# Moving stores of activated tiles and of prepared weight factors to GpSimd's queue, with two forms given later

## The chip, the cores and the metric

The kernel runs on one core of a Trainium2 chip. The core's engines are named as the profile names them: PE (TensorE matmul), PEld (its weight load), DVE (VectorE), ACT (ScalarE), POOL (GpSimd), SP (SyncE). "ACTq", "SPq" stand for what those engines' instruction queues do besides arithmetic, issuing DMAs above all. The metric is the device time of one execution in microseconds; the kernel before took 1059.97 us, the median of three runs (1058.99 to 1065.47).

## The reference

Three layers follow one another, in float32. First a retention over 4 batches, 8 heads, 768 positions and 64 features per head: a state per head is decayed and updated, and read with the query. The result, reshaped to 3072 tokens by 512 features, goes through two feed-forward layers of inner width 2048, the weights of which are given as 64-bit floats.

```python
state = gamma * state + k_t outer v_t          # y_t = scale * q_t @ state
x = y.transpose(0, 2, 1, 3).reshape(3072, 512)
h = x @ w_in;  x = np.maximum(0.01 * h, h) @ w_out        # first layer
h = x @ w_in2; y = (h * sigmoid(1.702 * h)) @ w_out2      # second layer
```

## The kernel before

A float32 product is made as three matmuls of values that are split into a rounded high part and the rest: ACT makes the high part (`nc.scalar.copy`), DVE subtracts it from the source. Layer products after the first columns are made by a seven-product scheme on half blocks (Strassen's manner): the products take sums of blocks, and those of the input are called forms 1 to 7.

The stages in order of time: the retention (`retention`, to about 134 us) with the first 512 columns of the first layer's inner products put between its steps (`ffn_in`, L244); a plain phase of 16 tiles (L948) for columns 512 to 767 by the same `ffn_in`; the first layer's input products by seven products (`first1`, class `First`, L533, to about 355 us); its output products (`second1`, class `Second`); and the same two for the second layer (`first2`, about 590 to 825 us, and `second2`).

In `First.run` the work goes over pairs (block of 768 columns, q of 8). A pair has seven groups of six matmuls of 384 columns each, and after each group comes a tick of a clock (`Later`), which calls steps that were put down for that tick; `beside` then calls at most one piece of the preparation of later weights (class `Prep`: a load, integer and float steps on ACT and DVE that turn 64-bit floats to float32, sums on DVE, a store). The first1 stage starts a `Prep` every 5 ticks, first2 every 7. Each engine runs its instructions in the order in which the program gives them. In a pair, `L672` is the ACT copy of the first product's PSUM bank to a second bank, and the later products into either bank come behind it. `inner` (L600) activates each of a pair's four results (`gate`, ACT, L618 for the gated layer and L620 for the other) into a tile of a ring of eight and stores it to DRAM (`store`, L608) on ACT's queue.

The DMA issues that the change touches: `factors_out` (L215, ACT; 8 times in the retention, the 512 KB tile `made` that POOL's subtractions of L157 write), `ffn_in`'s store (L257, ACT; in the retention and in the plain phase), `inner`'s store (L609, ACT) and `Prep.store` (L455, SP; 448 KB of prepared factors). SP's queue also issues the loads: L558 (a block of the layer's input, in four parts at the first block), L439 and L436 (raw weights), L898 (factors back from DRAM), L733 (activated tiles back for `Second`).

The forms of first1's first block are put down in the plain phase (`early_steps`, L941): form 7 at its last tile (L945), and form 3 in `step1` at the first pair (L958). `First.form` (L567) takes the ticks at which its subtraction of blocks, the ACT copy (L577) and the DVE subtraction come. The block sums that forms 5 and 6 start from are made by DVE at L563 and L565.

Of the kernel before, what the change touches and what calls it, by code (L numbers as in the profile page):

```python
# [22 lines left out]
B, H, S, D = 4, 8, 768, 64  # L23
# [4 lines left out]
TB = 512  # L28
# [3 lines left out]
NQ = KF // 2  # L32
# [58 lines left out]
def retention_two_ffn(ctx: ExitStack, tc: tile.TileContext, qkv, consts, small, w1i, w1o, w2i, w2o, scratch, out):  # L91
    nc = tc.nc
# [37 lines left out]
    wd = {kind: dram.tile([P, NQ, 2, 7, P], F32, name="wd" + kind) for kind in ("1o", "2i", "2o")}  # L130
    wdt = dram.tile([NQ, P, 4, QT], F32, name="wdt")
# [3 lines left out]
    later = Later()  # L135
# [76 lines left out]
    done = [0]  # L212

    def factors_out(q):
        nc.scalar.dma_start(out=wdt[q], in_=made)  # L215

    def work_first(n):
        if n + 2 < KF:
# [22 lines left out]
    h_banks = [7]  # L241
    i_h = [0]

    def ffn_in(m, x, cols, ring):  # L244
        n = cols.stop - cols.start
        h = banks[:, h_banks[i_h[0] % len(h_banks)], :n]
        i_h[0] += 1
        w = wt[m].rearrange("p s (k f) -> p s k f", k=NP)
        i = 0
        for k in range(NP):  # L250
            for a, c in ((0, 1), (0, 0), (1, 0)):
                nc.tensor.matmul(out=h, lhsT=w[:, a, k], rhs=x[c][:, k], start=(i == 0), stop=(i == 3 * NP - 1),  # L252
                                 skip_group_check=True)
                i += 1
        t = next(ring)[:, :n]
        nc.scalar.activation(out=t, in_=h, func=AF.Lrelu)
        nc.scalar.dma_start(out=gd1[m][:, cols], in_=t)  # L257

    def retention():
        in_ring = ring(run_of(ins_a, 4, 8), 4, 512)  # L260
# [159 lines left out]
    class Prep:  # L420
# [31 lines left out]
            subtract(f[:, 7], f[:, b21], f[:, 6], e)  # L452

        def store(self):
            nc.sync.dma_start(out=wd[self.kind][:, self.q, self.hh], in_=self.t[:, 1:])  # L455

        def steps(self):

# [74 lines left out]
    class First:  # L533
# [46 lines left out]
        def run(self, done, step, beside):  # L580
            later = self.clock

            def tick():
                later.tick()
                beside(self.free)

            nb = len(self.blocks)

            def product(t, n, i, start):
                blk, q = pairs[n]  # L590
                x = self.of[blk, i]
                w = self.weight(q, i)
                m = 0
                for k in range(2):
                    for a, b in ((0, 1), (0, 0), (1, 0)):
                        nc.tensor.matmul(out=t, lhsT=w(k, a), rhs=x[:, b, k], start=(start and m == 0),  # L596
                                         stop=(m == 5), skip_group_check=True)
                        m += 1

            def inner(n, r, f, src=None, made=None):  # L600

                blk, q = pairs[n]
                col, w = self.blocks[blk]
                cols = slice(col + r * w, col + (r + 1) * w)
                tile = lambda: next(self.g)[:, :w]
                ending = self.ending

                def store(t):  # L608
                    put = lambda: nc.scalar.dma_start(out=self.dst[f * NQ + q][:, cols], in_=t)  # L609
                    if ending:  # L610
                        self.pending.append(put)
                    else:
                        put()


                def gate(dst, src):
                    if self.gated:
                        nc.scalar.activation(out=dst, in_=src, func=AF.Gelu_apprx_sigmoid)  # L618
                    else:
                        nc.scalar.activation(out=dst, in_=src, func=AF.Lrelu)  # L620
                    if self.gated:
                        later.at(1, lambda: store(dst))
                    else:
                        store(dst)

                t = tile()
                if made is not None:
                    made(t)
                    later.at(1, lambda: gate(t, t))
                else:  # L630
                    gate(t, src)

            def add(o, x, y):
                nc.vector.tensor_tensor(out=o, in0=x, in1=y, op=ALU.add)  # L634

            pairs = [(blk, q) for blk in range(nb) for q in range(NQ)]
            state = {}
            for n in range(len(pairs) + 1):
                now = n < len(pairs)
                self.ending = not now  # L640
                step(n)
                cur, old = state.setdefault(n, {}), state.pop(n - 1, None)
                last = first_ = False
                if now:
                    blk, q = pairs[n]
                    w = self.blocks[blk][1]
                    last = q == NQ - 1 and blk + 1 < nb
                    first_ = q == 0 and blk > 0
                    if q == 1 and blk + 1 < nb:
                        parts = self.load(blk + 1)  # L650
                        for k, part in enumerate(parts):
                            later.at(7 * k * 4 // len(parts), part)
                    if q == 6 and blk + 1 < nb:
                        self.early_sums(0)
                        later.at(3, lambda: self.early_sums(1))
                self.free = not (last or first_ or n == 0)

                def form(i):
                    if last and i in FORMS[:4]:
                        self.form(blk + 1, i, (0, 2, 3) if i == 6 else (0, 1, 2))  # L660
                    if first_ and i in FORMS[4:]:
                        self.form(blk, i, (0, 2, 3) if i == 3 else (0, 1, 2))

                if now:
                    cur["a"] = self.bank("a", w)
                    product(cur["a"], n, 1, True)
                    cur["b"] = self.bank("b", w)
                    if n < len(self.p_banks["b"]):

                        nc.tensor.matmul(out=cur["b"], lhsT=self.weight(q, 1)(0, 0),  # L670
                                         rhs=self.of[blk, 1][:, 0, 0], start=True, stop=True, skip_group_check=True)
                    nc.scalar.copy(out=cur["b"], in_=cur["a"])  # L672
                    form(1)
                    tick()
                    cur["c"] = self.bank("c", w)
                    product(cur["c"], n, 5, True)
                    cur["p"] = next(self.p)[:, :w]
                    nc.scalar.copy(out=cur["p"], in_=cur["c"])
                    form(5)
                    tick()  # L680
                if old:
                    product(old["b"], n - 1, 7, False)
                    inner(n - 1, 1, 1, made=lambda t: add(t, old["b"], old["p"]))
                    form(7)
                    tick()
                if now:
                    product(cur["a"], n, 2, False)
                    inner(n, 0, 0, cur["a"])
                    form(2)
                    tick()  # L690
                    product(cur["b"], n, 6, False)
                    add(cur["c"], cur["b"], cur["p"])
                    form(6)
                    tick()
                if old:
                    product(old["c"], n - 1, 3, False)
                    inner(n - 1, 0, 1, old["c"])
                    form(3)
                    tick()
                    product(old["b"], n - 1, 4, False)  # L700
                    inner(n - 1, 1, 0, old["b"])
                    form(4)
                    done(*pairs[n - 1])
                    tick()
            later.drain()
# [231 lines left out]
    for part in first1.load(0):  # L937
# [4 lines left out]
                   4: lambda: (form(1, 0, 1, 2), factors[2].load()), 6: lambda: first1.early_sums(0),  # L942
                   7: lambda: (form(5, 0, 0, 1), first1.early_sums(1)), 9: lambda: form(2, 0, 0, 1),
                   10: lambda: factors[0].high(), 11: lambda: (factors[0].low(), form(6, 0, 1, 2)),
                   12: lambda: factors[1].high(), 13: lambda: (factors[1].low(), form(4, 0, 1, 2)), 15: lambda: form(7, 0, 0, 1)}  # L945
    tiles = [*range(NQ, KF), *range(NQ)]
    plain_g = ring(g_at[0], T1)
    for j, m in enumerate(tiles):  # L948
        ffn_in(m, x1, slice(TB, S), plain_g)
        if j in early_steps:  # L950
            early_steps[j]()
        later2.tick()
        beside(later2)

    def step1(n):
        if n == 0:
            apart[0] = 5
            form(3, 0, 1, 2)  # L958
            later2.at(3, factors[2].high)
            later2.at(4, factors[2].low)  # L960
        if n + 3 < NQ:
            factors[n + 3].load()
            later2.at(11, factors[n + 3].high)
            later2.at(12, factors[n + 3].low)
        if n == 17:
            first1.g = ring(g_at[1], T1)
        if n == 19:
            assert not todo
            second1.begin(later2, 0, NQ, 4, 24, 2)
# [258 lines left out]
```

## Time and profile before

| | |
|---|---|
| median of 3 runs | 1059.97 us (1058.99 to 1065.47) |
| the profiled execution's own time | 1061.2 us |
| its span, first to last instruction | 1059.5 us |
| mean granted TensorE clock | 0.995 |
| PE busy | 1027.5 us |
| DVE busy | 832.7 us |
| ACT busy | 620.8 us |
| POOL busy | 36.0 us |

The profile is one execution. Busy time does not count the issue of DMAs and waits in an engine's queue. The profiled execution took 1.7 us more than its span and 1.2 us more than the median of the runs.

### The profile page before, as it was taken

What the parts mean: (1) busy time and instruction counts of PE and PEld (TensorE: products, weight loads), DVE (VectorE), ACT (ScalarE), POOL (GpSimd) and SP (SyncE); (2) the same over time, 40 slices, a digit from 0 to 9 for tenths busy, and PEclk for the clock granted to TensorE, in tenths of its full rate; (3) what the DMA queues carried; (4) which work ended last, traced back from release to release, by engine and by line L of the source; (5) the groups of instructions that cost most, each with busy time, mean ns of one, the idle gap of its engine ahead of it and who ended that gap; (6) DMA issues with size and microseconds to landing.
All of it is one profiled execution on the core that took longest, in us unless ns stands there. A gap on an engine that the chain in (4) does not pass through costs nothing.

```text
span 1059.5 us, 17696 instructions
## 1 busy us (share of the span) xinstructions
PE 1027.5 (97%) x6197; PEld 913.5 (86%) x6198; DVE 832.7 (79%) x1479; ACT 620.8 (59%) x1256; POOL 36.0 (3%) x46
## 2 busy tenths in 40 slices
PE   8999997899999999999999899999999999999998
PEld 6777797899999788888887899999999888888886
DVE  5998749798873699899899648677655898887886
ACT  5766447676665666555546666565656654545453
POOL 2322200000000000000000000000000000000000
PEclk9999998999999999999999999999999999999999
DMA  9999888978868754834644656878578735725624
GB/s 329 346 361 405 301 259 273 338 265 311 298 209 302 261 162 139 291 115 155 246 158 150 256 208 209 283 233 268 202 244 284 247 100 121 197 83 146 170 80 80
DMA packets 186056, 240.55 MB, mean 227 GB/s; under 512 B 59376, under 2 KB 133872, under 8 KB 183792
## 3 DMA queue, kind: packets, MB, share of 16 engines
q1 hardware_dynamic: 143040, 184.06, 53.7%
q10 hardware_dynamic: 42928, 55.37, 14.4%
q8 instruction: 48, 0.79, 0.3%
q14 instruction: 40, 0.33, 0.1%
HBM read 145.53 MB, written 93.85 MB: 226 GB/s over the span
## 4 chain that ended last, share of the span: by engine, by line
PE 75%; DVE 8%; DMA 7%; ACT 5%; issue 3%; ACTq 2%; POOL 1%; SPq 0%; DVEq 0%
PE psum L788 39%; PE psum L596 28%; PE psum L252 4%; DMA h<-qkv 3%; DMA wd1o<-e 1%; PE psum L290 1%; DMA gd<-b 1%; ACTq L609 1%; PE psum L320 1%; DMA gd<-d 1%; DVE c L157 1%; DVE h L157 1%; POOL e L157 1%; PE psum L326 1%; PE psum L313 0%
## 5 line engine op out<-in xcount | busy, mean ns | idle before, releaser
L788 PE MATMUL psum<-c,h 128*128 128x512 f32 x1008 | 229.9, 390 | 4.5 <-DVE c L157 4.0
L788 PEld LDWEIGHTS psum<-c,h 128*128 128x128 f32 x1008 | 188.9, 188 | 45.2 <-DVE c L157 5.2
L788 PE MATMUL psum<-e,h 128*128 128x512 f32 x768 | 179.3, 389 | 0.0
L788 PEld LDWEIGHTS psum<-e,h 128*128 128x128 f32 x768 | 144.2, 188 | 29.9
L596 PE MATMUL psum<-c,h 128*128 128x384 f32 x576 | 110.4, 335 | 0.1
L596 PE MATMUL psum<-b,h 128*128 128x384 f32 x576 | 110.0, 334 | 0.0
L157 DVE TENSOR_TENSOR h<-h 128x256 fp32r<-128x256 f32 (+3 forms) x162 | 71.3, 482 | 40.7 <-ACT h L520 31.2
L596 PEld LDWEIGHTS psum<-c,h 128*128 128x128 f32 x576 | 100.6, 188 | 0.8 <-DVE d L634 0.8
L596 PEld LDWEIGHTS psum<-b,h 128*128 128x128 f32 x576 | 100.7, 188 | 0.0
L741 ACT CAST c<-b 128x512 fp32r<-128x512 f32 x96 | 59.4, 621 | 51.5 <-PE psum L788 27.2
L618 ACT ACTIVATE d<-psum 128x384 f32<-128x384 f32 x96 | 47.0, 492 | 71.3 <-PE psum L596 67.8
L596 PE MATMUL psum<-d,h 128*128 128x384 f32 x288 | 60.2, 344 | 14.5 <-ACT psum L672 14.0
L741 ACT CAST e<-a 128x512 fp32r<-128x512 f32 x77 | 47.7, 622 | 44.3 <-PE psum L788 21.8
L157 DVE TENSOR_TENSOR c<-b,c 128x512 fp32r<-128x512 f32 x96 | 65.0, 685 | 11.0 <-ACT c L741 10.0
L596 PE MATMUL psum<-f,h 128*128 128x384 f32 x336 | 67.5, 335 | 0.3 <-DVE e L634 0.3
L596 PEld LDWEIGHTS psum<-d,h 128*128 128x128 f32 x288 | 50.9, 191 | 17.8 <-ACT psum L672 17.8
L596 PEld LDWEIGHTS psum<-f,h 128*128 128x128 f32 x336 | 59.0, 188 | 1.0 <-DVE e L634 0.6
L596 PE MATMUL psum<-a,h 128*128 128x384 f32 x288 | 59.5, 343 | 0.0
L157 DVE TENSOR_TENSOR e<-a,e 128x512 fp32r<-128x512 f32 x77 | 52.2, 684 | 9.0 <-ACT e L741 8.4
L596 PE MATMUL psum<-e,h 128*128 128x384 f32 x288 | 58.1, 336 | 0.0
L596 PEld LDWEIGHTS psum<-a,h 128*128 128x128 f32 x288 | 52.7, 195 | 0.0
L596 PEld LDWEIGHTS psum<-e,h 128*128 128x128 f32 x288 | 51.1, 190 | 0.3 <-DVE e L157 0.3
(184 smaller groups left out, 1673.9 us busy)
## 6 DMA issues: line engine op xcount, KB each, us to landing
gd<-d ACTq DMA_DIRECT2D x160, 192.0 KB, 4.1
b<-gd SPq DMA_DIRECT2D x72, 256.0 KB, 4.2
d<-gd SPq DMA_DIRECT2D x72, 256.0 KB, 4.8
h<-qkv SPq DMA_DIRECT2D x17, 1024.0 KB, 8.6
a<-gd SPq DMA_DIRECT2D x48, 256.0 KB, 4.9
c<-w1i SPq DMA_DIRECT2D x16, 512.0 KB, 8.2
c<-w1o SPq DMA_DIRECT2D x32, 256.0 KB, 5.4
e<-w2o SPq DMA_DIRECT2D x32, 256.0 KB, 4.6
```

The lines of the kernel that those rows point to most:

```text
L157: e.tensor_tensor(out=o, in0=x, in1=y, op=ALU.subtract)
L252: nc.tensor.matmul(out=h, lhsT=w[:, a, k], rhs=x[c][:, k], start=(i == 0), stop=(i == 3 * NP - 1), skip_group_check=True)
L290: nc.tensor.matmul(out=ps[:, e, n], lhsT=kT[r, n], rhs=qT[r, n], start=True, stop=True, skip_group_check=True)
L320: nc.tensor.matmul(out=out(n, e), lhsT=v[:, n, r], rhs=sm[:, e, n], start=(n < 2), stop=(c == 0), skip_group_check=True)
L326: nc.tensor.matmul(out=out(n, e), lhsT=st[c % 2][r, n], rhs=q[r, n], start=False, stop=True, skip_group_check=True)
L596: nc.tensor.matmul(out=t, lhsT=w(k, a), rhs=x[:, b, k], start=(start and m == 0), stop=(m == 5), skip_group_check=True)
L609: put = lambda: nc.scalar.dma_start(out=self.dst[f * NQ + q][:, cols], in_=t)
L618: nc.scalar.activation(out=dst, in_=src, func=AF.Gelu_apprx_sigmoid)
L741: nc.scalar.copy(out=t[:, 0], in_=self.block_of(*item))
L788: nc.tensor.matmul(out=t[:, j], lhsT=w[:, j, a], rhs=x[:, b], start=(new and q == 0 and m == 0), stop=(q == NQ - 1 and m == 2), skip_group ...
```

## The change

Four DMA issues go to POOL's queue: `factors_out` and `First`'s stores from ACT's, `Prep.store` from SP's, and `ffn_in`'s from ACT's in the plain phase alone (in the retention it stays). The gated layer's store, which was put down for a tick later, is given at once. Form 7 of first1's first block, whose ACT copy came at the plain phase's last tile, comes at ticks 1 and 2 of the first pair; form 3's three steps come at ticks 4, 5 and 6 in place of 0, 1 and 2.

```diff
     def factors_out(q):
-        nc.scalar.dma_start(out=wdt[q], in_=made)
+        nc.gpsimd.dma_start(out=wdt[q], in_=made)
...
-    def ffn_in(m, x, cols, ring):
+    def ffn_in(m, x, cols, ring, queue=nc.scalar):
...
-        nc.scalar.dma_start(out=gd1[m][:, cols], in_=t)
+        queue.dma_start(out=gd1[m][:, cols], in_=t)
...
         def store(self):
-            nc.sync.dma_start(out=wd[self.kind][:, self.q, self.hh], in_=self.t[:, 1:])
+            nc.gpsimd.dma_start(out=wd[self.kind][:, self.q, self.hh], in_=self.t[:, 1:])
...
                 def store(t):
-                    put = lambda: nc.scalar.dma_start(out=self.dst[f * NQ + q][:, cols], in_=t)
+                    put = lambda: nc.gpsimd.dma_start(out=self.dst[f * NQ + q][:, cols], in_=t)
...
-                    if self.gated:
-                        later.at(1, lambda: store(dst))
-                    else:
-                        store(dst)
+                    store(dst)
...
-                   12: lambda: factors[1].high(), 13: lambda: (factors[1].low(), form(4, 0, 1, 2)), 15: lambda: form(7, 0, 0, 1)}
+                   12: lambda: factors[1].high(), 13: lambda: (factors[1].low(), form(4, 0, 1, 2))}
...
-        ffn_in(m, x1, slice(TB, S), plain_g)
+        ffn_in(m, x1, slice(TB, S), plain_g, nc.gpsimd)
...
         if n == 0:
             apart[0] = 5
-            form(3, 0, 1, 2)
+            form(7, 0, 1, 2)
+            form(3, 4, 5, 6)
```

## Rows read from the trace of the kernel before

**Rows 1.** Page, part 1: busy us (share of span) xinstructions of each engine
```profile
PE 1027.5 (97%) x6197; PEld 913.5 (86%) x6198; DVE 832.7 (79%) x1479; ACT 620.8 (59%) x1256; POOL 36.0 (3%) x46
```

**Rows 2.** Windows: stretch, us, busy (xcount) by engine, granted clock, DMA share, GB/s
```profile
0.00:140.00 140.00, 132.61 (x1667) 104.79 (x1669) 109.02 (x177) 82.82 (x236) 35.39 (x44) 1.00 0.94 340
140.00:158.40 18.40, 17.57 (x147) 17.37 (x146) 10.16 (x18) 8.65 (x19) 0.00 (x0) 1.00 0.89 286
158.40:205.00 46.60, 36.12 (x187) 35.16 (x186) 40.44 (x89) 30.45 (x64) 0.00 (x0) 0.90 0.91 305
205.00:250.00 45.00, 43.93 (x249) 43.01 (x248) 41.61 (x86) 31.36 (x62) 0.00 (x0) 0.99 0.81 270
250.00:360.00 110.00, 106.18 (x596) 102.88 (x595) 72.33 (x147) 68.00 (x137) 0.00 (x0) 1.00 0.78 272
...
603.00:825.00 222.00, 221.89 (x1278) 221.14 (x1277) 141.05 (x266) 138.67 (x281) 0.58 (x2) 1.00 0.72 244
```

**Rows 3.** Waits of PE: waiting line, releaser, us in total, times, longest us
```profile
PE psum L596 <- ACT psum L672: 14.0, 8, 6.2
```

**Rows 4.** Timeline, PE: start us, us, instructions [idle before, releaser]
```profile
166.98 2.29 PE L596 MATMUL psum<-d,h 128*128 128x384 f32 x6 [6.19 <-ACT psum L672]
...
172.40 1.21 PE L596 MATMUL psum<-d,h 128*128 128x384 f32 x6
...
190.56 1.31 PE L596 MATMUL psum<-d,h 128*128 128x384 f32 x6 [1.17 <-ACT psum L672]
...
201.22 1.61 PE L596 MATMUL psum<-d,h 128*128 128x384 f32 x6 [3.11 <-ACT psum L672]
```

**Rows 5.** Timeline, ACT, the end of the longest stall
```profile
165.35 0.33 ACTq L257 DMA_DIRECT2D gd<-d  x1
165.72 0.83 ACT L577 CAST e<-b 128x768 fp32r<-128x768 f32 x1 [0.40 <-ACT d L256]
166.46 0.47 ACT L672 COPY psum<-psum 128x384 f32<-128x384 f32 x1
```

**Rows 6.** Chain that ended last: start us, us, what
```profile
187.66 6.62 DMA wd1o<-e
...
194.30 0.02 ACTq L609
...
317.76 5.65 DMA gd<-d
...
323.44 0.02 ACTq L609
```

**Rows 7.** Lines L609 and L455: DMA issues, ns min/median/max, first and last start
```profile
L609 ACTq DMA_DIRECT2D gd<-d x160: 326/326/974, 176.2 to 829.1; - x160
...
L455 SPq DMA_DIRECT2D wd1o<-c x11: 319/339/599, 154.7 to 251.8; - x11
```

**Rows 8.** Waits of SP's queue, 140 to 150 us
```profile
SPq L558 <- DMA gd<-d: 2.9, 1, 2.9
SPq L558 <- DMA gd<-a: 2.6, 1, 2.6
```

**Rows 9.** Timeline, SP's queue: the fourth part of first1's first block
```profile
145.75 0.32 SPq L558 DMA_DIRECT2D b<-xd  x1
```

**Rows 10.** Timeline, DVE: the first sum of that block
```profile
150.68 0.96 DVE L563 TENSOR_TENSOR b<-b 128x768 f32<-128x768 f32 x1 [7.59 <-DMA gd<-a]
```

**Rows 11.** Windows, from that sum on
```profile
150.60:225.00 74.40, 62.79 (x353) 61.31 (x352) 66.27 (x141) 49.32 (x103) 0.00 (x0) 0.93 0.89 296
```

**Rows 12.** Waits, whole span: POOL
```profile
POOL e L157 <- DMA wdt<-e: 25.7, 3, 8.7
```

**Rows 13.** Timeline, DVE: one line beside POOL's work and without it
```profile
36.81 0.95 DVE L184 TENSOR_SCALAR g<-g 128x512 f32<-128x512 f32 x1
...
42.46 0.42 DVE L184 TENSOR_SCALAR b<-b 128x512 f32<-128x512 f32 x1
```

**Rows 14.** Timeline, POOL at that time
```profile
35.86 1.61 POOL L157 TENSOR_TENSOR e<-b,e 128x256 f32<-128x256 f32 x2
```

## The prediction, made before the result was known

> **What bounds the kernel now.** The engines' busy times come first: PE is busy 1027.5 of 1059.5 us [rows 1], so whatever the change gives must come out of some 32 us in which PE stands still, or out of time at a lower clock. The second view cuts the span into stages [rows 2]. PE's idle time is 7.4 us up to 140 us, 0.8 in the plain phase, 10.5 from 158.4 to 205, 1.1 to 250 and 3.8 to 360. From 603 to 825, where most of the moved stores lie, it is 0.1 us: there ACT's issue of stores is hidden entirely, and there is nothing to win. The stage to look at is therefore first1's start, where the granted clock is 0.90 as well.
>
> The third view says what PE waits for: the copy of line 672, 14.0 us in 8 waits [rows 3], of which 6.19, 1.17 and 3.11 us lie between 158 and 205 us [rows 4]. So ACT is late there, while it is busy only 30.45 of 46.60 us [rows 2]. The ACT timeline and the chain show why. Ahead of the copy stand a store and form 7's copy [rows 5]; a store costs ACT 0.326 us of issue [rows 7], and the instruction behind it starts 0.40 us after the one before [rows 5]. And stores wait in ACT's queue for other transfers to land: one until the factors' store of 187.66 us has landed, 6.62 us later, another 5.65 us for an earlier activated tile [rows 6]. Neither is data that the store needs. The same holds the other way: parts of first1's first block wait in SP's queue 2.6 and 2.9 us for ACT's stores to land [rows 8]; the last is issued at 145.75 [rows 9], and DVE's first sum on the block starts at 150.68, after 7.59 us of idle time [rows 10]. From there DVE works 66.27 of 74.40 us [rows 11]. So ACT and DVE go into first1 with a backlog, and PE pays.
>
> **The change part by part.** *Activated tiles' stores off ACT.* 224 issues of L609, of which the 96 of first1 lie where PE waits, and 16 of the plain phase: 112 x 0.40 = 45 us of ACT's queue up to 360 us, of which only what lies ahead of a late L672 counts. I take it that transfers of POOL's queue are not tied to the landings of the others, as those two queues are to each other; no row shows POOL's transfers, so the ends are: all of those waits gone, or none. I take them gone, since a wait now stands in a queue in which, after the retention, only stores stand.
>
> - Plain phase: 0 to 0.8 us; I take 0.5.
> - 158.4 to 205: PE's side allows its idle 10.5 us and the clock: the six matmuls after the long stall took 2.29 us against 1.21 [rows 4], and a mean clock of 0.90, a mix of the levels of 2.4 and 1.2 GHz, leaves at most 4.7 us in 46.6; I take 3, so 13.5 at most. DVE's side allows less. Without the waits of 2.6 and 2.9 us the block's sum starts some 5 us sooner, at 145.6; 66.3 us of work at 97% density (40.44 of the 46.6 us is 87%, with ACT's waits in it) end at 214 instead of 225, a gain of 11. At today's 89% [rows 11] only the 5 us remain. Between 5 and 11 I take 8.
> - 205 to 250: idle 1.1 us and 0.4 of clock; I take 0.7 of 0 to 1.5.
> - 250 to 360: 3.8 us; nearly every wait there ends with a store ahead of L672 or L620. A store's 0.40 is less than some of them; I take 2.5 of 1 to 3.8.
>
> *Prepared factors' store off SP.* 0.339 us of issue each [rows 7], and its wait for DVE's last sum no longer holds the loads behind it. Those loads are hidden by raw tiles loaded a `Prep` ahead; zero, and if a load were late, one L178 on ACT with it.
>
> *Factors of the retention.* ACT no longer stands behind POOL's sums. POOL already waits 25.7 us for these stores to land [rows 12] and will a little longer for its own; who needs its sums is the store alone. PE waits there mostly for loads at a DMA share of 0.94 [rows 2]; +0.5 us, between -1 and 1.5.
>
> *Gated stores given at once, and 603 to 825.* Covered by PE's 221.89 of 222 us; zero as long as POOL keeps up.
>
> *Forms.* Form 7's copy leaves the place ahead of L672 (0.74 us, counted in the 8). Form 3's low part now comes at tick 6, and its product follows tick 8, some 3 us later by 1.04 us a group; DVE's backlog is that long. A loss of 0 to 2 us; I take 1.
>
> *What is put on POOL.* A pair takes 222/1278 x 42 = 7.3 us [rows 2] and brings 4 + 7/5 = 5.4 stores in first1. So POOL may take 1.35 us for each. Bounds: ACT's 0.33 us below; above, no row. POOL's nearest instruction, a subtraction, takes 0.8 us (1.61 for two, rows 14); I take about 1 us, and POOL keeps up. Behind a store that waits for DVE stand up to five stores; ACT waits for them only when the ring of eight tiles, 14 us of work, is used up.
> The Trainium skill ("DMA: Bandwidth & Descriptors", Specifications) gives a first byte about 1 us after issue on this path against 0.6 on the others; no run here shows it yet, and by it the sum stays as it is.
>
> Sum: 0.5 + 8 + 0.7 + 2.5 + 0.5 - 1 = 11.2 us off the profiled execution's 1061.2 (a span of 1059.5 and 1.7 around it), so 1050.0. That execution is 1.2 above the median of the runs; against it the same gain gives **1049 us**. With all low ends 3 us are left, which is the rivals' ground, and the forecast ends at 5 (1055); with all high ends it is 18.6 us (1041.4), and since all at once is unlikely, it begins at 1042.
>
> **The rivals.** *Only the issue time is saved* (1055 us). If POOL's transfers are tied to the others as theirs are, the waits for landings stay. Then the longest stall gives three stores and form 7's copy, 3 x 0.40 + 0.74 = 1.9 us, and seven others one store each, 2.8: 5 us in all. For it: the rows show such ties between two queues [rows 6, 8]. Against it: the waiting store no longer stands ahead of ACT's work. Chance 0.14.
> The Trainium skill speaks for this one ("DMA: Bandwidth & Descriptors", Issuing engines are not separate DMA queues): issuing from several engines saves only the sequencer's issue time, usually small. The waits in rows 6 and 8 are a cost that this rule leaves out.
>
> *POOL's issuing slows DVE* (1057 us). DVE's L184 took 0.95 us while POOL subtracted, and 0.42 alone [rows 13, 14]. Each `Prep` has three such instructions; some 15 of them lie between 158 and 250 us, so 45 x 0.53 = 24 us if each met a store, where DVE is the second bound. A third of them gives 8 us, and 3 to 4 of the gain remain. Against it: no row shows POOL issuing a DMA, and it may hold nothing. Chance 0.15.
> The Trainium skill ("SBUF — State Buffer", SBUF: two separate sides) has the rule: a port pair shared by both, held for a whole instruction, and descriptors that POOL cannot write meanwhile. The rows agree for POOL's arithmetic; for its DMAs none shows it.
>
> *POOL is too slow* (1081 us, the side of slower). It decides from 1.35 us a store. At 1.6 us, first1's 24 pairs take 8.6 instead of 7.3 us, 32 us more, and 11 are won. Then ACT waits in L620 for a tile whose store hasn't landed. For it: POOL's instructions are the slowest here; against it: 0.8 us for the nearest. Chance 0.11.
>
> **How the numbers follow.** The forecast has 0.60, from 1042 to 1055. A measurement of this kernel tells about 1% (10.6 us) from no change, so faster means below 1049.4. Three quarters of the forecast's chance lie there, by my sum and its high ends: 0.45. The rest of it with the two middle rivals, 0.15 + 0.14 + 0.15, is 0.44 for the same. Slower is POOL's 0.11. The range, 1042 to 1062, takes in all but the last rival and some of DVE's worst.
>
> **What would show it.** In the changed trace: no DMA issue of L609 on ACTq; SP's L558 issues without a wait for gd; L563 at about 145 us; the 6.19 us stall down to 2 or less, and the granted clock near 1.00 from 158 to 205; POOL's issues about 1 us each; the stretch 603 to 825 unchanged. The prediction is wrong if PE waits for L672 as long as now with other causes ahead of it (DVE's forms above all), if L184 takes longer beside POOL's issues, or if L620 waits for tiles.

## The result: 12.6 us less, about what was forecast

The changed kernel takes 1049.61 us (median of 4 runs, 1048.79 to 1052.16) against 1062.18 (4 runs, 1058.99 to 1065.47) for the kernel before. The ratio is 0.9885, with a 95% interval of 0.9845 to 0.9926. The forecast was 1049, from 1042 to 1062. The ratio is a gain of 1.15%, and by the prediction's bound of 1% narrowly faster; the figure of 1049.4 us that the prediction worked out from this bound, with an earlier median of the kernel before, is missed by 0.2 us. The interval reaches to either side of the bound, so faster and same aren't told apart. The profiled execution takes 1050.06 us (a span of 1048.3), which is 11.1 less than the profiled execution before, and the sum had said 11.2; how far that is luck is said below.

In the changed kernel the line numbers behind L618 are smaller by three: L672 of before is L669, L634 is L631, L788 is L785, L898 is L895.

The first view is part 1 of the page of the changed kernel. PE is as busy as before in all [rows 1]; POOL's 158 us more are the issuing of stores: 290 instructions more, at some 0.54 us. Unlike ACT's and SP's, POOL's issues are counted as busy time.

```profile
PE 1026.7 (98%) x6198; PEld 914.6 (87%) x6198; DVE 835.6 (80%) x1479; ACT 616.3 (59%) x1256; POOL 194.7 (19%) x336
```

The second view is the windows of the changed kernel in the stretches of [rows 2] (stretch, us, busy and count by engine, granted clock, DMA share, GB/s).

```profile
140.00:158.40 18.40, 18.40 (x155) 18.40 (x155) 10.86 (x20) 10.42 (x24) 6.65 (x12) 1.00 0.96 342
158.40:205.00 46.60, 41.06 (x227) 40.42 (x226) 44.66 (x99) 32.21 (x68) 15.40 (x28) 0.96 0.90 319
205.00:250.00 45.00, 43.84 (x251) 43.23 (x251) 42.56 (x89) 31.26 (x63) 17.05 (x31) 1.00 0.84 288
250.00:360.00 110.00, 109.37 (x610) 106.19 (x609) 79.09 (x160) 69.83 (x148) 35.59 (x65) 1.00 0.82 291
...
603.00:825.00 222.00, 221.98 (x1264) 219.33 (x1263) 146.07 (x275) 135.64 (x277) 72.99 (x137) 1.00 0.70 241
```

From 158.4 to 205 PE's idle time falls from 10.5 us to 5.5, the granted clock rises from 0.90 to 0.96, and DVE works 44.66 of the 46.60 us where it worked 40.44. From 250 to 360 PE's idle time falls from 3.8 us to 0.6. From 603 to 825 nothing changes, as forecast.

Such fixed stretches hold other work in the two kernels, so the gain is better read from first1 itself, from its first six matmuls of L596 to the second stage's first matmul. These are windows of the kernel before and then of the changed one.

```profile
158.36:356.58 198.22, 182.85 (x1014) 178.24 (x1012) 153.31 (x316) 127.99 (x256) 0.00 (x0) 0.97 0.81 277
```

```profile
158.67:344.19 185.52, 178.19 (x1014) 176.49 (x1012) 152.36 (x314) 123.06 (x252) 67.32 (x123) 0.99 0.82 291
```

The same 1014 matmuls take 12.7 us less. 8.0 of this is PE's idle time (15.4 to 7.3), and 4.7 is its busy time, by the granted clock (0.97 to 0.99). The rest of the program gives a little back: first1 begins 0.3 us later, and what follows it takes 1048.3 - 344.2 = 704.1 us instead of 702.9.

The third view is what PE waits for from 140 to 360 us in the changed kernel, beside [rows 3].

```profile
PE psum L596 <- ACT psum L669: 2.9, 1, 2.9
PE psum L596 <- DVE e L157: 2.6, 1, 2.6
PE psum L596 <- DVE d L157: 1.2, 1, 1.2
```

Of eight waits for the copy of L669, 14.0 us in all, one of 2.9 us is left. The timeline of PE shows where the first two lie.

```profile
164.03 2.29 PE L596 MATMUL psum<-d,h 128*128 128x384 f32 x6 [2.94 <-ACT psum L669]
...
175.94 1.32 PE L596 MATMUL psum<-e,h 128*128 128x384 f32 x6 [2.60 <-DVE e L157]
```

The wait for d, 1.16 us, follows at 226.74. What stands ahead of the copy now is told by ACT's timeline.

```profile
160.09 0.84 ACT L577 CAST a<-b 128x768 fp32r<-128x768 f32 x1 [2.74 <-DVE b L157]
...
163.20 0.39 ACT L256 ACTIVATE d<-psum 128x256 f32<-128x256 f32 x1
163.48 0.50 ACT L669 COPY psum<-psum 128x384 f32<-128x384 f32 x1
```

No store stands there, and no DMA. ACT waited 2.74 us for DVE, so what is left of the stall is DVE's: the other bound that the prediction named. The chain of waits agrees: from 161.3 us on it runs from DVE's work to DVE's work until PE's second stall ends at 175.94.

Now the two other queues. First SP's timeline of the changed kernel at first1's first block, then DVE's first sum on that block, beside [rows 8 to 10].

```profile
139.61 2.32 SPq L558 DMA_DIRECT2D b<-xd  x4
142.03 9.09 SPq L895 DMA_DIRECT2D h<-wdt  x9
```

```profile
150.03 0.96 DVE L563 TENSOR_TENSOR b<-b 128x768 f32<-128x768 f32 x1 [6.09 <-DMA b<-xd]
```

The four parts of the block are issued in one go, the last at 141.24 instead of 145.75 us, and none of them waits for an ACT store to land. And yet DVE's sum begins at 150.03, only 0.65 us sooner.

Last POOL, in the view of lines: what its issues of stores take (ns min/median/max, first and last start), then two lines of DVE, the second of which is shown for the kernel before and then for the changed one.

```profile
L609 POOL DMA_DIRECT2D gd<-d x160: 539/539/609, 174.2 to 814.9; - x160
```

```profile
L184 DVE TENSOR_SCALAR c<-c x18: 408/420/498, 141.5 to 299.2; 128x512 f32<-128x512 f32 x18
```

```profile
L182 DVE TENSOR_SCALAR e<-e x16: 422/429/432, 634.0 to 771.1; 128x512 uint32<-128x512 uint32 x16
```

```profile
L182 DVE TENSOR_SCALAR e<-e x16: 423/515/527, 623.2 to 760.2; 128x512 uint32<-128x512 uint32 x16
```

A store costs POOL 0.54 us. DVE's L184 beside these stores keeps its median of 0.42 us, with 0.50 as the longest; L182 in first2 takes 0.52 us instead of 0.43. With the stores on SP's queue (a run below) its median is 0.430 us.

### The profile page after: what moved, and what is told of

It is laid out like the page before. It is cut to its first block, busy times and chain, and to the rows that moved or that the text cites. A ratio compares the mean times of both kernels' runs of the same rounds, so it can differ in the third digit from the quotient of the medians.

```text
span 1048.3 us, 17915 instructions
## 1 busy us (share of the span) xinstructions
PE 1026.7 (98%) x6198; PEld 914.6 (87%) x6198; DVE 835.6 (80%) x1479; ACT 616.3 (59%) x1256; POOL 194.7 (19%) x336
## 4 chain that ended last, share of the span: by engine, by line
PE 87%; DVE 6%; DMA 4%; issue 1%; ACT 0%; SPq 0%; DVEq 0%
PE psum L785 42%; PE psum L596 35%; PE psum L252 5%; DMA h<-qkv 3%; PE psum L290 2%; DMA h<-wdt 1%; PE psum L320 1%; DVE h L157 1%; PE psum L326 1%; PE psum L313 1%; DVE c L157 1%; DVE e L157 0%; DVE c L182 0%; DVE a L157 0%; DVE c L197 0%
## 5 line engine op out<-in xcount | busy, mean ns | idle before, releaser
L785 PE MATMUL psum<-c,h 128*128 128x512 f32 x1008 | 230.9, 391 | 4.6 <-DVE c L157 3.9
L785 PEld LDWEIGHTS psum<-c,h 128*128 128x128 f32 x1008 | 189.4, 188 | 45.5 <-DVE c L157 5.2
L785 PE MATMUL psum<-e,h 128*128 128x512 f32 x768 | 179.3, 389 | 0.0
L785 PEld LDWEIGHTS psum<-e,h 128*128 128x128 f32 x768 | 144.1, 188 | 29.9
L609 POOL DMA_DIRECT2D gd<-d x160 | 86.2, 541 | 425.6 <-ACT d L618 388.9
L596 PE MATMUL psum<-c,h 128*128 128x384 f32 x576 | 110.4, 335 | 0.0
L596 PE MATMUL psum<-b,h 128*128 128x384 f32 x576 | 110.0, 334 | 0.0
L596 PEld LDWEIGHTS psum<-c,h 128*128 128x128 f32 x576 | 100.6, 188 | 0.7 <-DVE d L631 0.6
L596 PEld LDWEIGHTS psum<-b,h 128*128 128x128 f32 x576 | 100.8, 188 | 0.0
L618 ACT ACTIVATE d<-psum 128x384 f32<-128x384 f32 x96 | 47.2, 492 | 72.9 <-PE psum L596 71.7
L596 PE MATMUL psum<-f,h 128*128 128x384 f32 x336 | 68.1, 337 | 0.0
L596 PE MATMUL psum<-d,h 128*128 128x384 f32 x288 | 58.8, 339 | 4.1 <-ACT psum L669 2.9
L596 PEld LDWEIGHTS psum<-f,h 128*128 128x128 f32 x336 | 59.8, 190 | 0.6 <-DVE d L631 0.3
L596 PE MATMUL psum<-e,h 128*128 128x384 f32 x288 | 57.6, 334 | 2.6 <-DVE e L157 2.6
L596 PE MATMUL psum<-a,h 128*128 128x384 f32 x288 | 58.1, 337 | 0.0
L596 PEld LDWEIGHTS psum<-d,h 128*128 128x128 f32 x288 | 51.3, 191 | 4.7 <-ACT psum L669 3.3
L596 PEld LDWEIGHTS psum<-e,h 128*128 128x128 f32 x288 | 50.5, 188 | 2.9 <-DVE e L157 2.9
```

What stands on the lines that cost most here:

```text
L609: put = lambda: nc.gpsimd.dma_start(out=self.dst[f * NQ + q][:, cols], in_=t)
L785: nc.tensor.matmul(out=t[:, j], lhsT=w[:, j, a], rhs=x[:, b], start=(new and q == 0 and m == 0), stop=(q == NQ - 1 and m == 2), skip_group ...
```

## The experiments

Theory A: ACT and SP lost time because each stood, in its own order of work, behind landings of the other's unrelated transfers; whatever takes the stores out of ACT's order ends that, and the issue time itself is worth little. Its rivals: B, the issue time is the gain; C, POOL's transfers are special and another queue wouldn't do; D, other parts of the change (the forms, the prepared factors' stores) carry it. Each time below stands against the kernel before on the same chip (1062.2 to 1062.65 us), as a median with the ratio and its 95% interval.

**The activated tiles' stores alone.** The kernel before with this part of the change:

```diff
-    def ffn_in(m, x, cols, ring):
+    def ffn_in(m, x, cols, ring, queue=nc.scalar):
...
-        nc.scalar.dma_start(out=gd1[m][:, cols], in_=t)
+        queue.dma_start(out=gd1[m][:, cols], in_=t)
...
-                    put = lambda: nc.scalar.dma_start(out=self.dst[f * NQ + q][:, cols], in_=t)
+                    put = lambda: nc.gpsimd.dma_start(out=self.dst[f * NQ + q][:, cols], in_=t)
...
-                    if self.gated:
-                        later.at(1, lambda: store(dst))
-                    else:
-                        store(dst)
+                    store(dst)
...
-        ffn_in(m, x1, slice(TB, S), plain_g)
+        ffn_in(m, x1, slice(TB, S), plain_g, nc.gpsimd)
```

> The kernel before with the activated tiles' stores alone on POOL's queue (first1, first2 and the plain phase); forms, factors and prepared factors as before. Theory (ACT's queue freed of issue time and of waits for landings): nearly all of the gain, 10 to 14 us less than before, and the waits of PE for line 672's copy fall from 14 us to 3 or less. Rival (only the issue time counts): 5 us less at most. Rival (the gain lies in the forms or in the prepared factors' store): within 2 us of before.

It took 1048.67 us, ratio 0.9879 (0.986 to 0.9899). This part gives as much as the whole change. PE's waits for the copy are down to 5.3 us in two (3 or less was expected), the longest of which stands in its timeline:

```profile
163.28 1.73 PE L596 MATMUL psum<-d,h 128*128 128x384 f32 x6 [4.29 <-ACT psum L669]
```

**The forms alone.** The kernel before with

```diff
-... 13: lambda: (factors[1].low(), form(4, 0, 1, 2)), 15: lambda: form(7, 0, 0, 1)}
+... 13: lambda: (factors[1].low(), form(4, 0, 1, 2))}
...
-            form(3, 0, 1, 2)
+            form(7, 0, 1, 2)
+            form(3, 4, 5, 6)
```

> The kernel before with the two forms given later and nothing else. Theory: form 7's copy ahead of the long stall is gone (0.7 us) and form 3's low part comes late (up to 2.6 us); between 1 us less and 2.5 us more than before. Rival (the forms carry the gain): 5 us less or better, with the 6.19 us stall down to 3.

It took 1060.09 us, ratio 0.999 (0.9975 to 1.0005): no difference. PE's waits for the copy are shorter here than in [rows 3], and form 3's later part takes back some of it; what is left of that, 2 us, doesn't show in the times.

```profile
PE psum L596 <- ACT psum L672: 10.4, 8, 5.2
PE psum L596 <- DVE e L157: 1.4, 1, 1.4
```

**The prepared factors' stores alone.** The kernel before with

```diff
-            nc.sync.dma_start(out=wd[self.kind][:, self.q, self.hh], in_=self.t[:, 1:])
+            nc.gpsimd.dma_start(out=wd[self.kind][:, self.q, self.hh], in_=self.t[:, 1:])
```

> The kernel before with the prepared factors' store alone moved from SP's to POOL's queue. Theory: ACT's stores no longer stand behind these stores' landings (two such waits, 2.3 and 1.4 us, lie on PE's path), but they find others; 0 to 4 us less than before. Rival (SP's loads, held by this store's waits, are what makes ACT and DVE late): 6 us less or better.

It took 1064.91 us, ratio 1.0019 (1.0005 to 1.0033): a loss of some 2 us (0.5 to 3.5) where a gain of 0 to 4 was expected. PE's waits for the copy are as in [rows 3]:

```profile
PE psum L596 <- ACT psum L672: 14.5, 7, 6.1
```

**The change with the forms as before.** The changed kernel with the forms' diff above undone.

> The changed kernel with both forms put back to where they were. Theory: the 2.60 us wait for form 3's low part goes, and form 7's copy comes back ahead of the copy that PE waits for first (0.7 us): 0 to 2 us less than the changed kernel. Rival (the forms help): 1 to 5 us more than the changed kernel, from a longer first stall.

It took 1049.77 us, ratio 0.9885 (0.987 to 0.9901), the same as the whole change. The stall at the copy is 1.1 us longer and form 3's stall of 2.60 us is gone:

```profile
165.13 2.29 PE L596 MATMUL psum<-d,h 128*128 128x384 f32 x6 [4.04 <-ACT psum L669]
```

The forms and the prepared factors' stores give nothing that can be told, and the stores alone, without the retention's factors, give all: these four leave D no ground.

**The issue time put back, without a transfer.** The changed kernel with a small copy on ACT behind each of the 112 stores of first1 and the plain phase:

```diff
                     store(dst)
+                    if not self.gated:
+                        nc.scalar.copy(out=dum, in_=dst[:, :64])
...
         queue.dma_start(out=gd1[m][:, cols], in_=t)
+        if queue is nc.gpsimd:
+            nc.scalar.copy(out=dum, in_=t[:, :64])
```

> The changed kernel with a small copy (64 columns, into a tile that nothing reads) given to ACT behind each store of first1 and of the plain phase, so that ACT's queue spends again about 0.3 to 0.4 us a store, without any wait for a transfer. Theory A (the landing waits in ACT's queue are the larger part of the gain): 1 to 4 us more than the changed kernel. Theory B (the issue time is the larger part): 6 to 11 us more than the changed kernel, near the kernel before.

It took 1050.7 us, ratio 0.9908 (0.9879 to 0.9937). That the dose was given is seen in the lines of this kernel and in its window over first1, where ACT is busy 145.98 us; the same window of the changed kernel has 123.51.

```profile
L626 ACT COPY dum<-a x33: 244/245/248, 167.0 to 344.4; 128x64 f32<-128x64 f32 x33
```

```profile
158.40:345.00 186.60, 178.87 (x1013) 176.23 (x1012) 151.62 (x313) 145.98 (x351) 68.29 (x124) 0.99 0.82 291
```

So 22.5 us more of work in ACT's queue, at the places where the issues stood, cost some 1 to 2.5 us. That tells against B, but the dose is only half of the 45 us that the prediction counts for 112 issues: taken in proportion, an estimate, the whole issue time would be worth 2 to 5 us.

**A small transfer on ACT's queue.** The changed kernel, its stores on POOL, with a DMA of 32 KB from ACT's queue at the same 112 places:

```diff
                     store(dst)
+                    if not self.gated:
+                        tiny()
...
         queue.dma_start(out=gd1[m][:, cols], in_=t)
+        if queue is nc.gpsimd:
+            tiny()
...
+    def tiny():
+        k = n_tiny[0]
+        n_tiny[0] += 1
+        nc.scalar.dma_start(out=scratch[k % 32][:, 0, 64 * (k // 32) : 64 * (k // 32) + 64], in_=dum)
```

> The changed kernel, with a small DMA of 32 KB (a tile of zeros to DRAM that nothing reads) issued from ACT's queue behind each store of first1 and of the plain phase: ACT's queue has its 112 issues again, and the ties to SP's transfers, but the stores stay on POOL. Theory A (waits for landings in ACT's queue are the larger part of the gain, tied between SP's and ACT's transfers): 5 to 12 us more than the changed kernel, clearly more than with the small copies, and PE waits again for line 669 (672 before). Theory B (the issue time, or the stores' own data): 1 to 3 us more, as with the small copies.

It took 1060.36 us (10 runs), ratio 0.9975 (0.9958 to 0.9992): 9.6 of the 12.2 us of gain are gone, by the ratios, though the activated tiles go out through POOL. Part of the chain that ended last (start, us, what) shows the mechanism in this kernel.

```profile
159.61 6.38 DMA c<-w1o
166.01 0.33 ACTq L142
166.34 0.04 issue
166.38 0.47 ACT psum L682
166.85 0.04 issue
166.90 2.30 PE psum L607 x6
...
184.40 6.39 DMA scratch<-dum
190.82 0.33 ACTq L142
```

L142 is the small DMA, L682 the copy that is L669 in the changed kernel, and c<-w1o a raw tile that SP loads. The small DMA has nothing to do with that tile, and yet it is issued only when the tile has landed. ACT is idle 1.16 us ahead of the copy at 166.38 and 1.57 us ahead of the next copy that is held so, at 191.24; PE waits 5.09 us for the first. The issue itself, 0.33 us, often costs ACT less here than a store's did, for the small DMA needn't wait for the activation that it stands behind and runs beside it, as in ACT's timeline:

```profile
137.66 0.38 ACT L265 ACTIVATE a<-psum 128x256 f32<-128x256 f32 x1 [2.66 <-PE psum L261]
137.66 0.33 ACTq L142 DMA_DIRECT2D scratch<-dum  x1
```

The other way round it is the same, in SP's waits and SP's timeline at the first block (L569 is L558):

```profile
SPq L569 <- DMA scratch<-dum: 4.3, 1, 4.3
```

```profile
140.32 6.91 SPq L569 DMA_DIRECT2D b<-xd  x4
```

The parts take 6.91 us to issue again, as they took some 7 before [rows 8, 9], and 2.32 with the change. What this run doesn't hold apart is the extra traffic of 112 x 32 KB = 3.6 MB: the DMA share from 158.4 to 205 us is 0.96 here and 0.90 with the change. From 159 to 201 us, though, the three transfers in the chain each release a small DMA in ACT's queue, and none releases DVE or PE.

**The same stores on SP's queue.** The changed kernel with

```diff
-                    put = lambda: nc.gpsimd.dma_start(out=self.dst[f * NQ + q][:, cols], in_=t)
+                    put = lambda: nc.sync.dma_start(out=self.dst[f * NQ + q][:, cols], in_=t)
...
-        ffn_in(m, x1, slice(TB, S), plain_g, nc.gpsimd)
+        ffn_in(m, x1, slice(TB, S), plain_g, nc.sync)
```

> The changed kernel with the activated tiles' stores on SP's queue in place of POOL's. ACT is as free as in the change; but SP's loads stand behind stores that wait for ACT, and loads and stores wait for each other's landings again. Theory (ACT's freedom is what counts, in first1 the loads have slack): 0 to 5 us more than the changed kernel. Rival (the queue must be one of its own): 8 us more or worse, with ACT or DVE waiting for raw weights or for the block's input.

It took 1048.5 us, ratio 0.9884 (0.9861 to 0.9908): as fast as on POOL. C falls. On SP the stores wait 134.9 us for ACT's tiles of first2, ahead of loads, and the time shows no cost of it.

```profile
SPq L609 <- ACT d L618: 134.9, 82, 5.1
```

**POOL made slower.** Three kernels, the changed one with 3, 6 and 14 small memsets on POOL behind each store of first1 and first2, to find from where POOL is too slow:

```diff
-                    put = lambda: nc.gpsimd.dma_start(out=self.dst[f * NQ + q][:, cols], in_=t)
+                    def put():
+                        nc.gpsimd.dma_start(out=self.dst[f * NQ + q][:, cols], in_=t)
+                        for _ in range(14):   # 3, 6
+                            nc.gpsimd.memset(dum[:, :8], 0.0)
```

> The changed kernel with 14 small memsets of some 0.1 us on POOL behind each of first1's and first2's stores (1.4 us more, so 4 x 1.4 + 5.4 x 0.54 = 8.5 us of POOL for a pair of 7.3 us). Theory (POOL decides from 1.35 us a store on average): 24 x 1.2 + 32 x 1.0 = 60 us more than the changed kernel, with ACT waiting in lines 620 and 618 for tiles whose store has not landed. Rival (the ring of eight tiles and the stages behind hide it): under 15 us more.

> As the run with 14 small memsets on POOL behind each activated store, with 3: about 0.5 us of memsets and 0.39 us of gap to the next issue, so 4 x 1.4 + 1.4 x 0.54 = 6.4 us of POOL for a pair of 7.3 us. Theory (POOL decides when its work for a pair passes 7.3 us): within 3 us of the changed kernel. Rival (any added delay of a store's issue shows): 8 us more or worse.

> The same with 6 memsets: about 1.0 us and 0.39 us of gap, so 4 x 1.93 + 0.76 = 8.5 us of POOL for a pair of 7.3 us in first1, 8.3 in first2. Theory: 24 x 1.2 + 32 x 1.0 = 60 us more than the changed kernel. Rival: under 20 us.

Fourteen took 1373.46 us, ratio 1.2942 (1.2909 to 1.2975), five times the loss expected, because the dose was larger: the memsets take 2.2 to 2.5 us by POOL's timeline instead of 1.4, and 0.39 us pass before the next issue.

Two others, sized by this, bracket the threshold. Three memsets took 1051.69 us, ratio 0.9894 (0.9866 to 0.9921), 2 us above the changed kernel by the medians and 1 by the ratios, which can't be told from nothing. Six took 1098.45, ratio 1.0342 (1.031 to 1.0373), which is 49 us more. Timelines of POOL, three and then six:

```profile
256.19 0.54 POOL L611 DMA_DIRECT2D gd<-a  x1 [0.39 <-ACT d L625]
256.72 0.45 POOL L613 MEMSET dum<- 128x8 f32 x3
```

```profile
262.93 0.54 POOL L611 DMA_DIRECT2D gd<-a  x1 [0.39 <-issue]
263.46 0.94 POOL L613 MEMSET dum<- 128x8 f32 x6
264.78 0.54 POOL L611 DMA_DIRECT2D gd<-d  x1 [0.39 <-issue]
```

With six a tile's store comes every 1.85 us. A pair has four of these and 1.4 stores of factors at 0.54, so 8.2 us of POOL's time against 7.3 of PE's, 1.5 us for each of 5.4 stores. With three it is 0.54 + 0.45 + 0.39 = 1.4 us, 6.3 us a pair and 1.2 for each. With six, ACT's L625 waits for a tile whose store hasn't landed, as the rival said:

```profile
ACT a L625 <- DMA gd<-a: 16.9, 4, 7.0
```

**Form 3 between its two places.** The changed kernel with

```diff
-            form(3, 4, 5, 6)
+            form(3, 2, 3, 4)
```

> The changed kernel with form 3 at ticks 2, 3 and 4 instead of 4, 5 and 6. Theory: the 2.60 us wait for its low part goes, and nothing else moves: 1 to 3 us less than the changed kernel. Rival (DVE is behind at that place whatever the order): the same time, the wait turns up at another form or sum.

It took 1049.05 us, ratio 0.9892 (0.9859 to 0.9924): the same, where 1 to 3 us less were expected. Form 3's stall is gone and three shorter ones have come: by PE's timeline up to 210 us, 0.44 and 0.73 us for DVE's L631, at 168.55 and 173.92 us, and 1.00 us for the copy, at 208.66. That fits the rival put down for this run, by which DVE is behind at that place whatever the order.

**Factors loaded later.** The changed kernel with form 3 as in the last one and the loads of two sets of factors, which stood around first1's first block in SP's queue, moved behind the ninth tile of the plain phase, to let the block land sooner:

```diff
-    early_steps = {1: lambda: factors[0].load(slice(2, 3)), 2: lambda: factors[1].load(),
-                   4: lambda: (form(1, 0, 1, 2), factors[2].load()), 6: lambda: first1.early_sums(0),
+    early_steps = {1: lambda: factors[0].load(slice(2, 3)),
+                   4: lambda: form(1, 0, 1, 2), 6: lambda: first1.early_sums(0), 8: lambda: (factors[1].load(), factors[2].load()),
...
-                   12: lambda: factors[1].high(), 13: lambda: (factors[1].low(), form(4, 0, 1, 2))}
+                   13: lambda: form(4, 0, 1, 2)}
...
-            form(3, 4, 5, 6)
+            form(3, 2, 3, 4)
+            later2.at(0, factors[1].high)
+            later2.at(1, factors[1].low)
```

> The changed kernel with form 3 at ticks 2 to 4, the loads of the second and third q's factors given at the plain phase's ninth tile (they were at its third and fifth, right behind first1's block in SP's queue), and the second's split moved into the first pair. Theory (the block's loads land late because they share the DMA engines with the nine factor loads issued behind them): DVE's first sum on the block at 147 us or earlier instead of 150.0, the first stall down from 2.9 to under 1.5 us, 2 to 4 us less than the changed kernel. Rival (the block's own bytes and the raw weights fill the engines): the sum starts as late as before, and the time is within 1.5 us, or worse by a late split.

It took 1048.41 us (1047.36 to 1052.06), ratio 0.9876 (0.9839 to 0.9912), not told apart from the change, where 2 to 4 us less were expected. The block's sum still waits 6.16 us for the landing, as DVE's timeline shows, and comes 10.4 us after the block's first issue (138.34 us), as in the changed kernel (139.61 to 150.03); the first stall is still 3 us. This was the try at a better version, and none of the five variants within the change's interval (this one, the stores alone, the old forms, form 3 between, SP's queue) can be called better.

```profile
148.78 0.96 DVE L563 TENSOR_TENSOR b<-b 128x768 f32<-128x768 f32 x1 [6.16 <-DMA b<-xd]
```

## Why the prediction was right, and which of its steps were not

**The place and the mechanism held.** The gain is in first1 (12.7 us by its windows; the prediction had 0.5 for the plain phase ahead of it, 8 + 0.7 + 2.5 for first1, and 1 off for form 3). That the activated tiles' stores in ACT's order of work are what cost it is shown in three ways: taken off ACT alone they give the whole gain, on SP's queue as well as on POOL's, and transfers put back on ACT's queue take most of it away. First1 by itself, in single profiles, says the same: 198.2 us before, 184.5 to 186.4 in the change and the five variants not told apart from it, 186.4 with the small copies and 194.9 with the small DMAs.

How the gain divides is less sure. Of the two runs with the same 112 places in ACT's queue, an instruction alone costs 1050.7 us, a transfer 1060.36. By the ratios against the changed kernel's 0.9885, the first gives back about 2.4 us (0.0023 of 1062) and the second about 7 more (0.0067); 2.6 us of the gain aren't given back by either. The intervals, 2 to 4 us either way, are as wide as the first and the last of these, the copies were half the dose, and the small DMAs bring traffic of their own. The trace of the kernel before fits. From 140 to 360 us ACT's timeline has 108 issues of stores, 37 us in all, and eight of these stand still for a landing first, 6.7 us in all. The longest such wait, 1.93 us, ends with the landing of the factors' store in [rows 6]; the 6.62 us there are that transfer's own time, not the wait.

```profile
191.90 0.49 ACT L620 ACTIVATE b<-psum 128x384 f32<-128x384 f32 x1 [1.00 <-PE psum L596]
194.35 0.33 ACTq L609 DMA_DIRECT2D gd<-b  x1
194.72 0.52 ACT L620 ACTIVATE d<-d 128x384 f32<-128x384 f32 x1 [2.33 <-DMA wd1o<-e]
```

Three of PE's eight waits come behind such stores, 1.17, 3.11 and 0.93 us. Behind the 3.11 us the granted clock was 0.83 from 201.2 to 211 us, which costs some 1.7 us, and in the changed kernel it is 1.00 there. So about 7 us for the landings is an estimate from rows, too. Ahead of the longest wait, 6.19 us, no store stood for a landing: with the stores off ACT and the forms as before it is 4.04 us, 2.15 less. The three issues of 0.40 us that stood there are 1.2 us of that; what the rest is, no run says. So the issue time is not nothing, and its share isn't measured. The Trainium skill ("DMA: Bandwidth & Descriptors", Issuing engines are not separate DMA queues) says that spreading DMAs over engines saves only issue time, usually small. The run with the copies doesn't contradict it on the issue time; the one with the small DMAs shows a cost that it leaves out, and by both estimates the larger one.

**The assumption that POOL's transfers are free of these ties held, for a wider reason.** In the changed kernel no wait of L609 on POOL ends with another transfer's landing; nearly all of them end with ACT's work. The run on SP shows that the queue needn't be one of its own: there the stores stand among loads, and the time is the same. What makes a DMA of ACT's queue wait for a landing of SP's was not tried.

**The step that failed is DVE's earlier start.** "The block's sum starts some 5 us sooner, at 145.6": it started at 150.03, 0.65 us sooner. The waits of 2.6 and 2.9 us in SP's queue are gone, as forecast, and the last part is issued 4.5 us sooner, but its landing is hardly earlier: from its issue to the sum it is 8.8 us instead of 4.9. The DMA engines are busy at a share of 0.95 in both kernels, as these windows show, from the first issue in the kernel before and from behind the last in the changed one; from the last issue to the sum alone it is 0.97 and 0.94. Nine loads of factors follow right behind the four parts.

```profile
138.90:150.70 11.80, 11.80 (x101) 11.80 (x100) 2.59 (x6) 4.04 (x9) 0.00 (x0) 1.00 0.95 305
```

```profile
142.00:150.70 8.70, 8.70 (x75) 8.70 (x74) 2.44 (x4) 2.27 (x5) 2.70 (x5) 1.00 0.95 357
```

The term of 8 us came near all the same, by its other half: DVE's density was to rise from 87% to 97%, and from 158.4 to 205 it is 44.66 of 46.60 us, 96%. From the block's sum on, the 66.3 us of DVE's work that took 74.3 us [rows 11] take 69.0 now:

```profile
150.03:219.00 68.97, 63.43 (x376) 62.47 (x375) 66.35 (x142) 48.67 (x105) 24.40 (x44) 0.98 0.92 325
```

That is 5.3 us from the density and 0.65 from the start, some 6 of the 8 taken and within the 5 to 11 given. DVE no longer waits for ACT's L178 there, 3.6 us from 150 to 205 in the kernel before; it didn't begin much sooner. What holds the block's landing back is open: with two of the three sets of factors loaded later, it took as long from its first issue.

**Sizes.** From 250 to 360 the idle time fell by 3.2 us (2.5 taken), from 205 to 250 it didn't fall (0.7 taken). Form 3 lost 2.60 us at its new place (1 taken, 0 to 2 given, so out of its bounds), and form 7's copy gave 1.1 at the first stall (4.04 against 2.94; 0.74 counted). In the times the two cancel: with the old forms 1049.77, with the new ones 1049.61. The prepared factors' stores were put at nothing; alone they cost 2 us (0.5 to 3.5). The plain phase takes 23.1 instead of 24.2 us, a gain of 1.1 (0.5 taken, 0.8 at most), the retention ends 1.4 us later (a gain of 0.5 taken, a loss of 1 at most), and what follows first1 lost 1.2 instead of 0. First1 begins between 156.74 us (form 3 between) and 160.85 (three memsets) in kernels that don't differ from the change in the retention, so these can't be told from chance by single profiles. That the sum of 11.2 met the profiled 11.1 is therefore partly luck: first1 gave 12.7 where the sum had 10.2, and all the rest lost 1.5 where it had a gain of 1.

**The rivals.** *Only the issue time* would have been 1055; it falls as the whole gain by the pair of runs above, and as 2 to 5 us of it, it isn't excluded. *POOL's issuing slows DVE* is true on a small scale and costs no time that shows: L182 in first2 goes from 0.43 to 0.52 us, L184's longest from 0.42 to 0.50, and DVE's total is 835.6 us against 832.7 before and 832.8 with the stores on SP; the L182 at 658.77 us, 0.52 us long, runs beside a store's issue from 658.50 to 659.04. The rival had 0.95 us for L184. Where POOL does arithmetic, in the retention, L184 still takes 0.95 us, so the share of the rule of the Trainium skill ("SBUF — State Buffer", SBUF: two separate sides) that concerns POOL's arithmetic agrees with the trace; beside POOL's issuing of DMAs a hold of 0.1 us at most shows in these lines, and a block for a whole instruction does not. *POOL is too slow* didn't come true, since a store costs 0.54 us and not the 1 that was taken; as a mechanism it is right: with the threshold worked out at 1.35 us a store, 1.2 costs nothing that can be told and 1.5 costs 49 us, through the tiles in L620's place.

**What it was not.** The prediction asked for a granted clock near 1.00 from 158 to 205 us and a first stall of 2 us or less; the clock is 0.96 and the stall 2.94. The six matmuls after that stall still take 2.29 us, as in [rows 4].

## What to carry to other kernels

Where an engine with work on the path also issues DMAs, read from the chain whether its issues wait for landings of transfers that they don't need; the price of an issue is then the wait in front of it as well as its own time. Move those issues to a queue that only moves data (which one didn't matter here), and count what one issue costs there against the pace at which they come: at 0.54 of 1.35 us, and even at 1.2, POOL was harmless, and at 1.5 it cost four times the gain. And a load that is issued earlier need not land earlier: issued 4.5 us sooner, at a DMA share of about 0.95, it landed 0.65 us sooner here.

## What the runs showed of the hardware that was not expected

- POOL issues a DMA of 192 KB in 0.54 us, minimum and median alike, against 0.33 on ACT [rows 7], and a DVE instruction of 0.43 us beside it takes up to 0.1 us longer. The transfers land in 4.3 us (median) after issue, those of ACT's queue before in 4.1. The Trainium skill ("DMA: Bandwidth & Descriptors", Specifications), by which, as an estimate, the first byte would come some 0.4 us later on this path, isn't contradicted by it, and the time didn't hang on it.
- A DMA of 32 KB on ACT's queue was nearly as harmful as one of 192 KB: its landing took 4.7 us (median), against 4.1 for the stores, and SP's queue waited 4.3 us for one. Its extra traffic is in that cost.
- Six small memsets (128x8) on POOL take 0.94 us, and 0.39 us pass between the last and the next DMA issue.
